# Attention with a two-matrix network: the multiplication by the softmax sums, moved from behind the visit to the middle of a slot

## The chip, the cores and the metric

The kernel runs on one core of one Trainium2 chip. The metric is device time in microseconds (us), from launch to end, of that core; lower is better. The core has five engines with instruction queues of their own: TensorE (PE; the loads of its weights are listed apart, as PEld), VectorE (DVE), ScalarE (ACT), GpSimd (POOL) and SyncE (SP), which here issues the DMAs. Each engine works through its queue in the order in which the program was written; between engines, semaphores make one wait for another.

## The reference, cut to what matters

Queries, keys and values have 8 batches, 12 heads, 448 positions and 64 numbers per head, all in float32. Queries and keys are normalised and weighted, then comes softmax attention, then a network of two matrices with `h - tanh(h)` between them:

```python
q_n, k_n = rmsnorm(q, g_q), rmsnorm(k, g_k)
scores = scale * (q_n @ k_n.T)
attn = exp(scores - max) ; attn = attn / (sum(attn) + 1e-9)
x = (attn @ v)            # as 3584 rows of 768
h = x @ w_in              # 768 x 2048
out = (h - tanh(h)) @ w_out   # 2048 x 768
```

The sum of the exponentials divides the product with the values, not the exponentials: `x` is `exp(scores) @ v`, multiplied by the sum's reciprocal.

## The kernel before, in words

The work is cut into 48 steps: step `s` is one batch `b = s // 6` and one pair of heads `hp = s % 6`. Attention of one step gives `xT`, a tile of 128 rows (64 for each of the two heads' numbers, in an order of the kernel's own) and 448 columns, the positions. Six of these tiles are a batch's input to the network.

The network of an earlier batch runs beside the attention of a later one. It is written as a generator (`mlp`), which yields after every matmul, and a function `run(ns)` takes as many of its matmuls as fill so many nanoseconds. So the order of the program is fixed when it is built: a slot of attention writes a few attention instructions, calls `run`, writes the next few, and so on. No scheduler moves anything after that.

The network multiplies with a scheme of seven products for a 2 x 2 block product (Winograd's form of Strassen's), so that its matmuls come as products of a few matmuls each, every product into one bank of PSUM. Three banks, called `mm`, serve all of them in turn. A product's bank has to be read by ScalarE or VectorE before another product may write it or add to it. In the hidden layer (`hidden`, matmuls at L841) these reads are L908 (ScalarE), L910, L912, L920, L916, L917 and L924 (VectorE), and the subtraction of the tanh, L889, on VectorE for one product in seven and on GpSimd for three. In the projection of two batches at once (`project_pair`, matmuls at L1094) they are the lines of `add`, L1101, on VectorE, and L1174, L1168 and L1108 on ScalarE; L1042 on VectorE and L1051 on GpSimd make sums of blocks of the network's activations for later products.

From step 12 on, a step is handled by `slot(s)`. It begins with a "visit": from step 13 (`FOLDED`) on, all matmuls of this step's values (L623, L635) and of the next step's scores (L569) in one go, with the exponentials (L575) on ScalarE. The visit's result lies in two banks; `divide` adds them into `xT` (ScalarE copies the first, L757; VectorE adds the second, L758) and multiplies each half of 64 rows by `rs`, the reciprocals of the sums (L762, twice). Behind the visit stand fourteen points with the network's matmuls before, between and behind them, evenly by time. At the points the slot writes what the next steps need. The first three add the exponentials of step `s + 1` (L600, L606, L613 twice, all VectorE). The fourth and fifth turn and sum them (L710, L717). The sixth scales queries and keys of step `s + 2` (L530). At the seventh stand copies on ScalarE (L725, the first half, and L501), at the eighth VectorE's transpose of the queries (L540) and the other half of L725, at the ninth the transpose of the keys (L544) and a sum (L508). The tenth has the last sums and their reciprocals (L733, L734), the twelfth and thirteenth spread and turn them into `rs` for the next slot (L741 on ScalarE, L747 on VectorE). GpSimd has the power of step `s + 2` (L523) directly behind the visit, and sums of `xT` tiles (L793, `x_sums`) in the slots of a batch's last two steps.

A slot with `hp` of 0 to 3 runs beside a hidden layer, one with 4 or 5 beside a projection; slots 28, 29, 40 and 41 are about twice as long as the others.

Of the kernel before, what the change touches and what calls it, by code (L numbers as in the profile page):

```python
# [13 lines left out]
ALU = mybir.AluOpType  # L14
# [132 lines left out]
def bounded_path(tc, ctx, q, k, v, moe_w_in, moe_w_out, out, g_col, ident, ones, half_ones, neg_half, early):  # L147
# [17 lines left out]
    nc = tc.nc  # L165
    B, H, S, D = q.shape
# [3 lines left out]
    NP = H // 2  # L170
# [328 lines left out]
    def square_blocks(s):  # L499
        sq = normed["sq", s] = late["blocks"].tile([P, 2 * S], F32, name="sum_T")  # L500
        nc.scalar.activation(  # L501
            sq, loaded["qk", s].rearrange("p i j d -> p (i j d)"), AF.Square
        )
# [31 lines left out]
    def turn_blocks(s, i):  # L535

        n = normed[s][:, i].rearrange("p j d -> p (j d)")
        if i == 0:
            qT = qkp.tile([P, S], F32, name="qT")
            nc.vector.transpose(out=qT, in_=n)  # L540
            turned[s] = qT
            return
        kT = qkp.tile([P, S], F32, name="kT")
        nc.vector.transpose(out=kT, in_=n)  # L544
        turned[s] = None, kT, turned[s]
        del normed[s]
# [5 lines left out]
    def sc_bank():  # L552
        return bank_of("sc")

    def scores(s, c, apart=False):

        rr, kT, qT = turned[s]
        n = S if c < KF else HS
        name, bufs = ("p", 2) if c < 2 else ("p_full", 1) if c < KF else ("p_last", 2)
        if c == 1:  # L560
            p = probs[s, 1] = probs[s, 0]
        else:
            p = probs[s, c] = pp.tile([P, 2, 2 if c < 2 else 1, n], F32, name=name, bufs=bufs)
        tiles = [sc_bank() for _ in range(2)]

        def score(h, i):
            at, first = (i * BL, 0) if c < KF else (i * BL % KR, i * BL // KR * n)
            r = slice(h * D, (h + 1) * D)
            nc.tensor.matmul(  # L569
                tiles[h][i * BL : (i + 1) * BL, :n], lhsT=kT[r, c * P + at : c * P + at + BL],  # L570
                rhs=qT[r, first : first + n], start=True, stop=True,
            )

        def exp(h):
            nc.scalar.activation(  # L575
                p[:, h, c if c < 2 else 0, :], tiles[h][:, :n], AF.Exp,
                scale=1.0 if rr is None else rr[:, 0, 2 * c + h : 2 * c + h + 1],
            )

        if apart:  # L580
            return [(lambda i, h=h: score(h, i), lambda h=h: exp(h)) for h in range(2)]
        for i in range(P // BL):
            for h in range(2):
                score(h, i)
        for h in range(2):
            exp(h)
# [5 lines left out]
    def add(s, now=True):  # L592

        if s <= NP + NP // 2:
            sums[s] = []
            return
        t = early["sum"]
        sums[s] = [t]
        p = full(s)
        nc.vector.tensor_tensor(out=t, in0=p[0], in1=p[1], op=ALU.add)  # L600
        if now:
            add_third(s)
# [118 lines left out]
    def gather(s, h):  # L721

        acc, part = whole[s], whole["part", s]
        for g in range(P // BL):
            nc.scalar.copy(  # L725
                out=acc[h * BL : (h + 1) * BL, g], in_=part[g * BL : (g + 1) * BL, h * NJ : (h + 1) * NJ]
            )
# [21 lines left out]
    def divide(s, av):  # L749
        b, hp = steps[s]  # L750
        rs = whole.pop(s)
        if b > PAIRED and b % 2 and hp == 1:
            x = xT[b, hp] = late["blocks"].tile([P, S], F32, name="xT_more", bufs=1)
        else:
            x = xT[b, hp] = xp.tile([P, S], F32, name="xT")
        if s >= FOLDED:
            nc.scalar.copy(out=x, in_=av[0][:, :S])  # L757
            nc.vector.tensor_tensor(out=x, in0=x, in1=av[1][:, :S], op=ALU.add)  # L758
        for m in range(2):
            rows = slice(m * D, (m + 1) * D)  # L760
            if s >= FOLDED:
                nc.vector.tensor_tensor(out=x[rows], in0=x[rows], in1=rs, op=ALU.mult)  # L762
                continue
            for n in range(2):
                nc.vector.tensor_tensor(
                    out=x[rows, n * HS : (n + 1) * HS], in0=av[n][rows, :HS], in1=rs[n * D : (n + 1) * D],
                    op=ALU.mult,
                )
        for c in range(NCH):
            del probs[s, c]  # L770
        if b < PAIRED and hp >= HC:
            c = hp - HC
            x_sums(b, (c,), range(4), nc.vector if b == 0 and c == HC - 1 else nc.gpsimd)

    def x_sums_later(s, second):
        b, hp = steps[s]
        for c in {(HC + 1, 1): (0,), (HC + 1, 2): (1,), (HC + 2, 0): (2,)}.get((hp, second), ()):
            x_sums(b, (c,), range(4), nc.gpsimd)

    def x_sums(b, chunks, which, eng):  # L780

        for c in chunks:
            x11, x12, x21, x22 = (xT[b, r][:, n : n + HS] for r in (c, c + HC) for n in (0, HS))
            for i in which:
                if i != 2 and (b, i) not in tt:
                    tt[b, i] = tp.tile([P, HC, HS], F32, name=f"tt{i}", bufs=1)
                out, a, z = (
                    lambda: (tt[b, 0][:, c], x12, x11),
                    lambda: (tt[b, 1][:, c], x22, tt[b, 0][:, c]),
                    lambda: (x12, x22, x12),  # L790
                    lambda: (tt[b, 3][:, c], x21, tt[b, 1][:, c]),
                )[i]()
                eng.tensor_tensor(out=out, in0=a, in1=z, op=ALU.subtract)  # L793


    late = {}
# [517 lines left out]
    def gap_ns(s):  # L1314

        if s < 2 * NP:
            return H_NS / 12 if s % NP < 3 else 4 * S / ENGINE_NS * CD * CF / 12
        if s < 3 * NP:
            return (H_NS + O_NS + AHEAD_NS) / (4 * NP)
        n = (s - 3 * NP) % (2 * NP)  # L1320
        return (H_NS / 16, OUTER_NS * SOON / 8, H_NS / 16, OUTER_NS * (len(OUTER) - SOON) / 8)[(n > 3) + (n > 5) + (n > 9)]

    def has(s):
        return 0 <= s < NS

    def first_slot(s):
# [31 lines left out]
        if has(s):  # L1358
            divide(s, av)
# [34 lines left out]
    def slot(s):  # L1394

        gap = gap_ns(s)
        av = av_banks
        if has(s + 1):
            scores(s + 1, KF)
        if s < FOLDED:  # L1400
            last_values(s, av)
            totals(s, sc_bank())
            divide(s, values(s, av))
            for c in range(KF):
                scores(s + 1, c)
        else:
            visit(s, av)
        if has(s + 2):
            load(s + 2, "v")
        rows, ahead, following = has(s + 2), has(s + 3), has(s + 1)  # L1410
        folded = following and s + 1 >= FOLDED
        first = s + 3 == TURNED
        scaled = rows and not first
        if scaled:
            power_blocks(s + 2)
        work = (
            (
                (following, lambda: add(s + 1, False)), (first, lambda: turn(s + 2, sc_bank(), sc_bank())),
                (ahead and not first, lambda: load_blocks(s + 3)),
            ),  # L1420
            (
                (following, lambda: add_third(s + 1)), (first, lambda: load_blocks(s + 3)),
                (True, lambda: x_sums_later(s, 0)),
            ),
            ((following, lambda: add_last(s + 1)),),
            ((folded, lambda: fold(s + 1)),),
            ((folded, lambda: fold_rest(s + 1)), (True, lambda: x_sums_later(s, 1))),
            ((scaled, lambda: scale_blocks(s + 2)),),
            ((folded, lambda: gather(s + 1, 0)), (ahead, lambda: square_blocks(s + 3))),
            ((scaled, lambda: turn_blocks(s + 2, 0)), (folded, lambda: gather(s + 1, 1))),  # L1430
            ((scaled, lambda: turn_blocks(s + 2, 1)), (ahead, lambda: norm_blocks(s + 3))),
            ((folded, lambda: spread_sums(s + 1)), (True, lambda: x_sums_later(s, 2))),
            ((scaled, lambda: weigh_keys(s + 2)), (ahead, lambda: meet_blocks(s + 3))),
            ((folded, lambda: widen_sums(s + 1)),),
            ((folded, lambda: turn_sums(s + 1)),),
            (),
        )
        for point in work:
            run(4 * gap / (len(work) + 1))
            for wanted, fn in point:  # L1440
                if wanted:
                    fn()
        run(4 * gap / (len(work) + 1))
# [358 lines left out]
```

## Time and profile before

Median of three runs: 1359.16 us (1357.87 to 1359.49). The profile is of one further execution:

| What | Value |
|---|---|
| Profiled execution, device time | 1356.19 us |
| Its span, first to last instruction | 1354.4 us |
| Granted TensorE clock over the span | 0.996 |
| TensorE, VectorE, ScalarE, GpSimd busy | 97%, 70%, 41%, 57% |
| L762, the two multiplications | 70 of them, 58.5 us |
| VectorE idle before the 35 L758 | 195 us |
| Chain that ended last | 84% TensorE, 9% VectorE, 2% DMA, 2% SyncE's queue |

In the profile's rows a line number with an engine names a group of instructions, `out<-in` are the tiles written and read, and a shape such as 64x448 is partitions by elements. Behind a bar or in square brackets stands the time in which the engine was idle before, and what ended most of that. "Waits" rows give the total in us, how many times, and the longest. Rows in order of time begin with the start and the duration in us.

### The profile page before, as it was taken

To read this page: it belongs to the slowest core of one execution; us is meant where nothing else is said; L and a number is where in the kernel's file an instruction comes from. 1 tells how busy PE (TensorE), PEld (TensorE's weight loads), DVE (VectorE), ACT (ScalarE), POOL (GpSimd) and SP (SyncE) were. 2 spreads that over 40 slices of the span, in tenths; PEclk is the share of its full clock that TensorE was granted. 3 is DMA by queue.
4 is the path that set the end of the run, shared out by engine and by line. 5 is a ranking of instruction groups with operands and counts; after the bars stand their busy time and mean duration, and the time that the engine had idled before them with its cause. 6 is when DMAs were issued, how large, how long until landed. Compare 5 with 4: busy or idle time off the path is not lost.

```text
span 1354.4 us, 29206 instructions
## 1 busy us (share of the span) xinstructions
PE 1317.9 (97%) x11336; PEld 1029.0 (76%) x11336; DVE 949.1 (70%) x1393; ACT 556.9 (41%) x1326; POOL 775.1 (57%) x591
## 2 busy tenths in 40 slices
PE   7989999999999999999999999999999999999996
PEld 3467854478998878697778787778787888699985
DVE  4999978757855768587887576768786668434453
ACT  7856654344433454445322446354512264311100
POOL 4766766347846256626698235844699253712761
PEclk9999999999999999999999999999999999999999
DMA  7879889889999667476655867476645775365544
GB/s 172 197 198 266 254 256 254 249 247 280 335 302 274 169 157 182 107 192 151 162 145 138 197 169 179 110 180 163 168 139 139 160 194 158 107 163 178 171 143 84
DMA packets 371688, 253.54 MB, mean 187 GB/s; under 512 B 282196, under 2 KB 310228, under 8 KB 371540
## 3 DMA queue, kind: packets, MB, share of 16 engines
q1 hardware_dynamic: 371536, 251.57, 68.9%
q8 instruction: 92, 1.51, 0.5%
q14 instruction: 56, 0.46, 0.1%
q10 hardware_dynamic: 4, 0.00, 0.0%
HBM read 205.23 MB, written 46.27 MB: 186 GB/s over the span
## 4 chain that ended last, share of the span: by engine, by line
PE 84%; DVE 9%; DMA 2%; SPq 2%; issue 1%; ACT 1%; POOL 1%; DVEq 0%; ACTq 0%
PE mm L841 36%; PE mm L1094 23%; PE sc L569 9%; PE sc L635 6%; PE mm L1258 5%; DVE xT L762 1%; PE sc L673 1%; PE sc L623 1%; SPq L955 1%; PE mm L673 1%; DVE rows L613 1%; DMA w_f<-w_in 1%; DVE rows L606 1%; DVE rows L600 1%; DMA w_f<-w_inner 0%
## 5 line engine op out<-in xcount | busy, mean ns | idle before, releaser
L841 PE MATMUL mm<-xT,w_f 128*128 128x224 f32 x1296 | 264.0, 353 | 0.7 <-DVE s L912 0.7
L841 PEld LDWEIGHTS mm<-xT,w_f 128*128 128x128 f32 x1296 | 244.5, 190 | 6.4 <-issue 4.8
L569 PE MATMUL sc<-qT,kT 64*32 64x448 f32 (+1 forms) x3072 | 214.2, 499 | 2.9 <-ACT p_last L575 1.7
L841 PE MATMUL mm<-tt,w_f 128*128 128x224 f32 x1044 | 213.7, 356 | 0.8 <-DMA w_f<-w_in 0.2
L841 PEld LDWEIGHTS mm<-tt,w_f 128*128 128x128 f32 x1044 | 194.9, 190 | 19.1 <-issue 15.4
L523 POOL TENSOR_TENSOR rr_mine<-rr_mine,neg_half 128x28 f32<-128x28 f32 x33 | 160.6, 4868 | 2.7
L758 DVE TENSOR_TENSOR xT<-xT,sc 128x448 f32<-128x448 f32 x32 | 19.9, 622 | 176.8 <-PE sc L569 119.3
L889 POOL TENSOR_TENSOR gT<-s,th 128x448 f32<-128x448 f32 x44 | 56.1, 1277 | 145.3 <-ACT th L888 142.0
L1094 PE MATMUL mm<-u,w_f 128*128 128x224 f32 x672 | 136.5, 354 | 1.2 <-DVE sum_all L733 0.9
L1094 PE MATMUL mm<-gT,w_f 128*128 128x224 f32 (+1 forms) x480 | 133.0, 429 | 3.1 <-DVE acc L1101 3.0
L1094 PEld LDWEIGHTS mm<-u,w_f 128*128 128x128 f32 x672 | 126.1, 190 | 8.2 <-POOL u L1051 3.9
L569 PEld LDWEIGHTS sc<-qT,kT 64*32 64x32 f32 x3072 | 71.0, 106 | 70.4 <-issue 50.5
L1094 PEld LDWEIGHTS mm<-gT,w_f 128*128 128x128 f32 x480 | 90.2, 190 | 40.7 <-issue 34.2
L635 PE MATMUL sc<-p,v_nat 64*32 64x448 f32 x1120 | 110.5, 536 | 0.0
L1094 PE MATMUL mm<-g,w_f 128*128 128x224 f32 (+1 forms) x360 | 99.5, 428 | 1.1 <-DVE acc L1101 1.1
L725 ACT COPY sum_g<-sum 32x14 f32<-32x14 f32 x280 | 56.3, 201 | 106.1 <-DVE sum L717 100.3
L889 POOL TENSOR_TENSOR g<-s,th 128x448 f32<-128x448 f32 x24 | 30.6, 1278 | 108.2 <-ACT th L888 93.3
L575 ACT ACTIVATE p<-sc 128x448 f32<-128x448 f32 x132 | 71.7, 543 | 50.3 <-PE sc L569 42.4
L1094 PEld LDWEIGHTS mm<-g,w_f 128*128 128x128 f32 x360 | 67.9, 190 | 28.2 <-issue 26.2
L1258 PE MATMUL mm<-gT,w_out 128*128 128x448 f32 x192 | 74.4, 543 | 0.0
L1051 POOL TENSOR_TENSOR u<-gT 128x448 f32<-128x448 f32 x48 | 58.8, 1247 | 11.1 <-PE mm L1094 11.1
L144 POOL TENSOR_TENSOR rr<-rr,neg_half 112x8 f32<-112x8 f32 (+1 forms) x30 | 49.4, 1675 | 26.7 <-DVE rr L143 26.2
(196 smaller groups left out, 2427.9 us busy)
## 6 DMA issues: line engine op xcount, KB each, us to landing
w_f<-w_in SPq DMA_DIRECT2D x196, 384.0 KB, 3.5
w_f<-w_inner SPq DMA_DIRECT2D x63, 512.0 KB, 3.7
w_f<-w_out SPq DMA_DIRECT2D x42, 512.0 KB, 3.9
w_raw<-in_moe_w_out_dram SPq DMA_DIRECT2D x16, 768.0 KB, 5.6
w_in<-w_out SPq DMA_DIRECT2D x21, 384.0 KB, 5.1
qk_nat<-in_q_dram SPq DMA_DIRECT2D x132, 56.0 KB, 2.8
qk_nat<-in_k_dram SPq DMA_DIRECT2D x132, 56.0 KB, 2.3
g<-w_out SPq DMA_DIRECT2D x14, 512.0 KB, 5.1
```

Of the source, the lines that this page charges most:

```text
L144: nc.gpsimd.tensor_tensor(out=r, in0=r, in1=neg_half[:rows], op=ALU.pow)
L523: nc.gpsimd.tensor_tensor(out=mine, in0=mine, in1=neg_half[:, :1].to_broadcast([P, 2 * NJ]), op=ALU.pow)
L569: nc.tensor.matmul(tiles[h][i * BL : (i + 1) * BL, :n], lhsT=kT[r, c * P + at : c * P + at + BL], rhs=qT[r, first : first + n], start=True ...
L575: nc.scalar.activation(p[:, h, c if c < 2 else 0, :], tiles[h][:, :n], AF.Exp, scale=1.0 if rr is None else rr[:, 0, 2 * c + h : 2 * c + h ...
L635: nc.tensor.matmul(av[g][i * BL : (i + 1) * BL, :S], lhsT=v_nat[keys, h, c, m * BL : (m + 1) * BL], rhs=p[keys, h], start=first, stop=True ...
L673: nc.tensor.matmul(av[n][r : r + BL, :HS], lhsT=v_nat[:, h, c, m * BL : (m + 1) * BL], rhs=p[c][:, h, n * HS : (n + 1) * HS], start=False, ...
L725: nc.scalar.copy(out=acc[h * BL : (h + 1) * BL, g], in_=part[g * BL : (g + 1) * BL, h * NJ : (h + 1) * NJ])
L841: nc.tensor.matmul(bank[:, f * HS : (f + 1) * HS], lhsT=w[:, c * width + f, :], rhs=moving[p](c), start=(first and f == 0 and c == 0), sto ...
L889: eng.tensor_tensor(out=g[:, rows, cols], in0=h, in1=th, op=ALU.subtract)
L1051: nc.gpsimd.tensor_tensor(out=u[:, half], in0=a[:, half], in1=z[:, half], op=ALU.subtract)
L1094: nc.tensor.matmul(bank[:, :n], lhsT=w(i), rhs=mv, start=(first and i == 0), stop=(i == len(moving) - 1), skip_group_check=not first,)
L1258: nc.tensor.matmul(bank[:, :S], lhsT=w_out_row(f, n // HC)[:, n % HC * P : (n % HC + 1) * P], rhs=g[:, f, :], start=(f == 0), stop=(f == C ...
```

## The change: the two multiplications are written at the seventh and eighth point

`divide` no longer multiplies, except where `hp` is 5, a batch's last step. For all others it puts two functions, one for each half of 64 rows, on a list, and a slot's seventh and eighth point each take one from it and call it. In a batch's last step both are called at once, as before. The multiplications themselves, their tiles and all other instructions stay.

```diff
         if s >= FOLDED:
             nc.scalar.copy(out=x, in_=av[0][:, :S])
             nc.vector.tensor_tensor(out=x, in0=x, in1=av[1][:, :S], op=ALU.add)
+            for m in range(2):
+                rows = x[m * D : (m + 1) * D]
+                late.setdefault("divide", []).append(
+                    lambda rows=rows: nc.vector.tensor_tensor(out=rows, in0=rows, in1=rs, op=ALU.mult)
+                )
         for m in range(2):
             rows = slice(m * D, (m + 1) * D)
             if s >= FOLDED:
-                nc.vector.tensor_tensor(out=x[rows], in0=x[rows], in1=rs, op=ALU.mult)
+                if hp == NP - 1:
+                    divide_rows()
                 continue
...
+    def divide_rows():
+        if late.get("divide"):
+            late["divide"].pop(0)()
...
-            ((folded, lambda: gather(s + 1, 0)), (ahead, lambda: square_blocks(s + 3))),
-            ((scaled, lambda: turn_blocks(s + 2, 0)), (folded, lambda: gather(s + 1, 1))),
+            (
+                (folded, lambda: gather(s + 1, 0)), (ahead, lambda: square_blocks(s + 3)),
+                (True, divide_rows),
+            ),
+            (
+                (scaled, lambda: turn_blocks(s + 2, 0)), (folded, lambda: gather(s + 1, 1)),
+                (True, divide_rows),
+            ),
```

The points' own work of VectorE is written in this order from then on: L530 at the sixth, the first multiplication at the seventh, L540 and then the second multiplication at the eighth, L544 at the ninth.

## The prediction

> **What bounds the kernel now.** I read the page first, then who waits for whom on the weight-load queue between 300 and 1200 us (the stretch that holds every slot the diff touches), then slots in order of time. "Slot 46" is step 46: batch 7, head pair 4; offsets count from the start of its L758.
>
> ```profile
> PE 1317.9 (97%) x11336; PEld 1029.0 (76%) x11336; DVE 949.1 (70%) x1393; ACT 556.9 (41%) x1326; POOL 775.1 (57%) x591
> ```
>
> TensorE sets the end. Its 97% cannot be read as "no stalls", because ends of matmuls are modelled; the weight loads, one per matmul, show them:
>
> ```profile
> PEld mm L1094 <- DVE acc L1101: 7.0, 8, 2.1
> PEld mm L841 <- DVE gT L889: 1.4, 3, 0.5
> PEld mm L841 <- DVE s L912: 1.4, 2, 0.7
> PEld mm L841 <- DVE g L889: 1.0, 2, 0.5
> PEld mm L1094 <- DVE s L1101: 0.9, 3, 0.4
> PEld mm L841 <- DVE s L917: 0.9, 5, 0.2
> ```
>
> With L920 (0.5, 1), L600 (0.4, 2) and L1042 (0.2, 1), TensorE waited for VectorE 27 times, 13.7 us. Loads of 128x224 matmuls stand 0.19 us apart anyway, so 27 x 0.19 = 5.1 of it is no loss: 8.6 remain. After nearly each, the second matmul starts 0.10 late, some 2 us in all. So late VectorE reads of product banks cost about 10.5 us of 1354.4: the most that the change can win. The worst slot, VectorE's rows and then the weight loads':
>
> ```profile
> 1160.38 0.62 DVE L758 TENSOR_TENSOR xT<-xT,sc 128x448 f32<-128x448 f32 x1 [6.99 <-PE sc L569]
> 1161.04 2.79 DVE L762 TENSOR_TENSOR xT<-xT,rs_T 64x448 f32<-64x448 f32 x2
> 1163.85 0.39 DVE L1101 TENSOR_TENSOR acc<-mm,s 128x224 f32<-128x224 f32 x1
> 1164.16 1.60 DVE L600 TENSOR_TENSOR rows<-p 128x896 f32<-128x896 f32 x1
> ...
> 1170.77 0.35 DVE L1101 TENSOR_TENSOR acc<-mm,acc 128x224 f32<-128x224 f32 x1
> ```
> ```profile
> 1164.30 1.43 PEld L1094 LDWEIGHTS mm<-gT,w_f 128*128 128x128 f32 x8 [1.05 <-DVE acc L1101]
> 1166.17 2.94 PEld L1094 LDWEIGHTS mm<-u,w_f 128*128 128x128 f32 x16 [0.45 <-issue]
> 1171.17 0.30 PEld L1094 LDWEIGHTS mm<-gT,w_f 128*128 128x128 f32 x2 [2.06 <-DVE acc L1101]
> ```
>
> VectorE has idled 7 us for the visit, then gets a burst. L1101 reads a bank filled before the visit, but stands behind the two L762; three times TensorE waits for a bank (the 0.45, called "issue", starts as the L1101 of 1165.68 ends). In a hidden-layer slot, one more read matters:
>
> ```profile
> 618.63 1.27 DVE L762 TENSOR_TENSOR xT<-xT,rs_T 64x448 f32<-64x448 f32 x2
> 633.45 0.61 DVE L917 TENSOR_TENSOR s<-mm,s 128x448 f32<-128x448 f32 x1
> ```
> ```profile
> 626.80 0.30 PEld L841 LDWEIGHTS mm<-xT,w_f 128*128 128x128 f32 x2 [0.74 <-DVE s L912]
> 629.47 2.19 PEld L841 LDWEIGHTS mm<-tt,w_f 128*128 128x128 f32 x12 [0.48 <-DVE g L889]
> 634.11 0.68 PEld L841 LDWEIGHTS mm<-tt,w_f 128*128 128x128 f32 x4 [0.18 <-DVE s L917]
> ```
>
> Here VectorE never idles from L758 to L917, and TensorE goes on as L917 ends.
>
> **What the Trainium skill says.** "SBUF — State Buffer", Who interferes with whom: a VectorE instruction with two SBUF inputs contends with a GpSimd one that reads SBUF, one with a single SBUF input does not. The trace agrees: L762 takes 0.62 alone and 1.3 to 1.6 beside GpSimd's L1051 or L1005, L600 1.09 or 1.60; L910, one input in PSUM, stays 0.62 beside L1051. The long power of L523 does not slow them: slot 34's L600 took 1.08 under it. "PSUM — Partial Sum Buffer", Engine vs sequencer instructions: VectorE's queue is strictly in order; the burst above shows it. "Perfetto Trace Analysis", Identifying the Most-Contended Engine: matmul busy share is no measure of headroom; the stalls under 97% agree.
>
> **The change, part by part.** Nothing is removed or added: 70 L762 before and after. Six slots of the 35 are a batch's last and keep theirs; 29 x 2 = 58 move behind L530 and behind L540 (in long projection slots among the L1042). The other four engines' order does not change; no DMA moves. Two GpSimd sums (L793) gain a wait on VectorE.
>
> At the old place everything up to L530 moves up by the pair's time, 1.3 us where GpSimd is quiet, up to 3.1 where it is not. At the new place the backlog is what it was, as long as VectorE has not idled meanwhile. So a stall before the new place goes for good only if no read behind it binds, or if the pair has become cheaper there. Stalls with their restarts, taken from gaps between matmul starts over 0.19:
>
> Slot 46, 0.97 + 0.37 + 1.97 = 3.3. The first L1101 ends at 1.05 instead of 3.86, L600 takes its 1.6, the second ends at 2.9, L606 and L613 stay slow beside GpSimd, the third ends at 7.9 instead of 10.74. The product that started at 10.80 starts at 8.0, after GpSimd's last u (6.37 before) has held one by 0.4. No later read is short. Gain 2.8.
>
> Slots 22 and 34, 0.91 and 0.85: the first L1101 ends at 1.05, not 3.2; the third near 6.2, not 8.2; VectorE idles 1.2 before L747 there. Gain 1.76.
>
> Slots 28 and 40, 1.34 and 0.67. The L1101 behind three L1042 (offsets 23.4 and 23.8) comes behind an L762 too: 0.65 to 1.45 later. Its bank is needed 1.5 and 0.75 after its old end, and TensorE now comes 1.3 and 0.7 earlier. I take 1.1 and 0.2: 1.3.
>
> Slots 20, 32 and 44, 0.4 before L889 and 0.1 before L917, each. Their pairs took 2.9 beside L1051; at offsets 9 to 12 GpSimd is idle (3 to 13.7), so they take 1.24, 1.7 less, while L600 and L606 now meet L1051 and grow by 0.65. L917 comes 1.0 earlier, TensorE 0.5. Gain 1.45.
>
> Slots 26 and 38, 1.06 and 0.98: their pairs were cheap already (1.27), so L917 ends where it did and takes all of it back. Gain 0. The other 19 moved slots have no stall that an L762 makes; slot 18's L917 ends 1.2 before it is needed, slot 33's 0.6.
>
> Sum 2.8 + 1.76 + 1.3 + 1.45 = 7.3. For the reads behind point eight that come later than the hand count sees I take off 0.8 (bounds: 0, and all but slot 46's, 4.5). **Gain 6.5 us.** The profiled execution (span 1354.4, 1356.19 with what lies around) becomes 1349.7; the median shown, 3.0 above it, 1359.16 - 6.5 = 1352.7. Behind slot 46 TensorE runs 147 us of matmuls almost without a gap, so a gain there reaches the end.
>
> What the moved pair holds up: behind it stand L540, L544 and L508 (used a slot later), L920 to L924 (product banks, counted above), L733, L734 and L747 (the next sums; needed only after the next visit). ScalarE's copies for the sums wait for L717, which comes earlier. L793's second group stands at point ten: in slot 46 GpSimd reaches it at 14.78, the pair is done near 13; cost 0, and if it waited GpSimd's next u would be late by the wait, at most about 1 us.
>
> **Rivals.** *All stalls go*: TensorE wins the whole of the slots counted, 3.3 + 1.76 + 2.01 + 1.5 + 2.04 = 10.6: 1348.6. For it: the reads behind point eight often have 0.6 to 1.2 of slack. Against it: slots 26 and 38 have none. *The stalls move*: L917 and the L1101 behind L1042 take back everything except part of slot 46: gain 0 to 2.7, about 1357.7. For it: five L917 waits stand in the list already. Against: GpSimd is idle where the pair goes in slots 20, 32 and 44. *Slower*: the pair, now between L530 and L544, runs contended or meets a VectorE that idled earlier, and L917 comes late in hidden slots. The seven with no slack (20, 26, 27, 32, 38, 39, 44) lose 1.7 each and ten like slot 18 or 33 lose 0.5 to 1.1: 12 + 8 = 20, less 6 won in the projections: up to 14, as a middle value 3.5: 1362.7. It decides once the pair costs over 1.2 more in its new place. Against: in slots 26 and 32 GpSimd is idle there, from 6 or 3 to 14. *It doesn't do what it says* is excluded: the instruction order shows the move.
>
> **How the numbers follow.** Forecast (gain over 2.7, up to 9.5): 0.59, its own range 1350 to 1356. All stalls go: 0.11. They move: 0.14. Slower: 0.16. A change under 0.2%, 2.7 us, cannot be told from none. Faster 0.59 + 0.11 = 0.70, same 0.14, slower 0.16. The range leaves out a tenth at each side: it takes in nearly all of the first rival and the milder part of the slower one, 1348.3 to 1360.
>
> **What would show it.** Waits of loads for L1101 fall from 7.0 to about 2; slot 46's product of 1171.17 starts 8.0 behind its L758; L762 falls from 856 ns mean to 700 to 750, L600 rises above 1202; L889 and L912 vanish from the list and L917 stays in slots 26 and 38. It is wrong if L917, or L1101 behind L1042, grows by as much as the others fall, if L762 stays above 850, or if GpSimd waits for L762.

## The result and the profile after

The changed kernel takes 1355.24 us (median of 22 runs) against 1357.59 of the kernel before (22 runs beside it): 0.9983 of the time, 95% interval 0.9976 to 0.999. That is 2.35 us less, where the prediction had 6.5. Its profiled span is 1352.9 us, 1.5 less. (One of the 22 runs of the kernel before took 1692.89; without it the median is 1357.38.) From here on a line number of the changed kernel is 10 higher than the same statement's in the kernel before, from L793 on: L917 is L927, L889 is L899, L912 is L922, L1042 is L1052, L1051 is L1061, L1101 is L1111; L762, L600, L606 and L613 keep theirs.

The page's first part, as after:

```profile
PE 1315.2 (97%) x11336; PEld 1030.8 (76%) x11336; DVE 958.5 (71%) x1393; ACT 559.0 (41%) x1326; POOL 792.8 (59%) x591
```

No instruction was added, yet VectorE is busy 9.4 us longer (949.1 before) and GpSimd 17.7 (775.1 before). So some work takes longer: the first sign that the move changed what runs beside what. The waits on the weight-load queue between 300 and 1200 us, of the changed kernel:

```profile
PEld mm L1104 <- POOL u L1061: 7.4, 9, 1.2
...
PEld mm L851 <- DVE s L927: 2.9, 2, 1.5
PEld mm L1104 <- DVE acc L1111: 1.9, 3, 1.5
PEld mm L1104 <- DVE s L1111: 1.3, 3, 0.6
PEld mm L851 <- DVE xT L762: 0.9, 1, 0.9
...
PEld mm L851 <- DVE g L899: 0.5, 2, 0.3
```

The same view of the kernel before has, beside the lines that the prediction showed, these of GpSimd:

```profile
PEld mm L1094 <- POOL u L1051: 3.7, 5, 0.7
PEld mm L1094 <- POOL g L889: 1.6, 2, 0.8
PEld mm L1094 <- POOL rr_mine L520: 1.5, 2, 0.7
```

The large wait, 7.0 for the `acc` of L1101, is down to 1.9, and L912 is gone. Two others took part of it. The wait for L917's statement grew from 0.9 to 2.9, all of it now in two places, slots 26 and 38. The wait for GpSimd's `u` grew from 3.7 to 7.4. Of that, 1.5 is a change of name: in slots 22 and 34 the wait of 0.73, as the network's loads resume behind the visit, stood under L520 before. The other 2.3 are new, in slots 28 and 40. The 1.6 under GpSimd's L889, in slots 27 and 39, is L917's too: in slot 27 of the kernel before L917 ends at 655.46 and the load starts at 655.57, while L889 had ended at 654.90.

Waits alone do not give the loss, so I use one ledger for every kernel here: the gaps between the starts of successive network matmuls beyond their usual spacing (0.19 us for 128x224, 0.38 for 128x448), summed by slot. The 0.10 us by which the second matmul behind every visit starts late, before and after, is left out. A slot's length is the distance from its L758 to the next. Before, the stalls of slots 13 to 47 sum to about 13.5 us, after to 2.8 less. (The span has only 1.5 of these 2.8: the profiled execution after is 0.8 later at slot 13 already, ahead of everything that was moved, and 0.5 longer behind slot 47.) By slot, lengths in us:

| Slots | Before | After | Gain | Predicted gain |
|---|---|---|---|---|
| 46 | 23.56 | 21.67 | 1.9 | 2.8 |
| 22, 34 | 23.09, 23.00 | 22.18, 22.15 | 1.76 | 1.76 |
| 20, 32, 44 | 22.05, 21.97, 21.97 | 21.52, 21.50, 21.50 | 1.47 | 1.45 |
| 28, 40 | 48.41, 47.82 | 48.15, 48.21 | -0.13 | 1.3 |
| 26, 38 | 22.65, 22.64 | 23.07, 23.14 | -0.92 | 0 |
| 23, 35 (keep their pair) and 27, 39 | 22.48, 22.54; 22.30, 22.18 | 22.68, 22.71; 22.37, 22.24 | -0.5 | -0.8, as the allowance |

These sum to 3.6. Another 0.8 is lost in three slots: slot 14 loses 0.39 and slot 42 0.81, while slot 30 gains 0.40. In slot 30 of the kernel before, and in slot 42 of the changed one, a matmul starts 0.135 us behind the landing of a transfer of weights. The wait above for L762 is this place in slot 42. Such late weights stand now in one slot and now in another.

Slot 14 looks like another in the first profile of the changed kernel, where one matmul starts 0.135 behind a landing. But a second profile of that kernel loses the same 0.39 there, without that late matmul. VectorE's pair before, then VectorE, GpSimd and the load of the second profile:

```profile
334.21 1.27 DVE L762 TENSOR_TENSOR xT<-xT,rs_T 64x448 f32<-64x448 f32 x2
```
```profile
346.42 1.69 DVE L762 TENSOR_TENSOR xT<-xT,rs_T 64x448 f32<-64x448 f32 x1
...
349.21 1.74 DVE L762 TENSOR_TENSOR xT<-xT,rs_T 64x448 f32<-64x448 f32 x1
350.97 0.63 DVE L899 TENSOR_TENSOR gT<-mm,th 128x448 f32<-128x448 f32 x1
```
```profile
345.51 6.57 POOL L1015 TENSOR_TENSOR g<-g 128x512 f32<-128x512 f32 x4
```
```profile
351.65 0.86 PEld L851 LDWEIGHTS mm<-tt,w_f 128*128 128x128 f32 x5 [0.34 <-DVE gT L899]
```

The pair took 0.62 for each half behind the visit. At its new place it meets GpSimd's L1015 and takes 3.4 us. L899, the read behind it, ends late, and the load waits for it. So this loss is the move's own. It is the one slot where TensorE waits because the moved pair has itself become dearer.

Slot 46 of the changed kernel in order of time, VectorE and then the weight loads:

```profile
1160.30 0.62 DVE L758 TENSOR_TENSOR xT<-xT,sc 128x448 f32<-128x448 f32 x1 [6.88 <-PE sc L569]
1160.84 0.38 DVE L1111 TENSOR_TENSOR acc<-mm,s 128x224 f32<-128x224 f32 x1
1161.14 1.70 DVE L600 TENSOR_TENSOR rows<-p 128x896 f32<-128x896 f32 x1
...
1163.06 1.72 DVE L606 TENSOR_TENSOR rows<-rows,p_full 128x896 f32<-128x896 f32 x1
1164.82 2.91 DVE L613 TENSOR_TENSOR rows<-rows,p_last 64x448 f32<-64x448 f32 x2
...
1168.80 0.35 DVE L1111 TENSOR_TENSOR acc<-mm,acc 128x224 f32<-128x224 f32 x1
```
```profile
1164.68 3.03 PEld L1104 LDWEIGHTS mm<-u,w_f 128*128 128x128 f32 x16
1169.21 0.30 PEld L1104 LDWEIGHTS mm<-gT,w_f 128*128 128x128 f32 x2 [1.49 <-DVE acc L1111]
```

The burst behind the visit has lost its L762, and the first L1111 follows L758 at once. But the three sums of exponentials now take 6.3 us for 5.3 before: they moved beside GpSimd's `u`. The third L1111 ends 8.85 behind L758 (10.74 before), and the product waits 1.49 instead of 2.06.

Slot 26 shows the opposite sign. Before, its L606 and L613:

```profile
621.47 1.50 DVE L606 TENSOR_TENSOR rows<-rows,p_full 128x896 f32<-128x896 f32 x1
623.00 2.09 DVE L613 TENSOR_TENSOR rows<-rows,p_last 64x448 f32<-64x448 f32 x2
```

After, with GpSimd and the weight load that waits:

```profile
620.14 1.08 DVE L606 TENSOR_TENSOR rows<-rows,p_full 128x896 f32<-128x896 f32 x1
621.26 2.92 DVE L613 TENSOR_TENSOR rows<-rows,p_last 64x448 f32<-64x448 f32 x2
...
629.42 0.61 DVE L762 TENSOR_TENSOR xT<-xT,rs_T 64x448 f32<-64x448 f32 x1
...
631.13 0.62 DVE L762 TENSOR_TENSOR xT<-xT,rs_T 64x448 f32<-64x448 f32 x1
...
633.83 0.62 DVE L927 TENSOR_TENSOR s<-mm,s 128x448 f32<-128x448 f32 x1
```
```profile
620.37 3.33 POOL L1061 TENSOR_TENSOR u<-g 128x448 f32<-128x448 f32 x2
```
```profile
634.50 0.68 PEld L851 LDWEIGHTS mm<-tt,w_f 128*128 128x128 f32 x4 [1.47 <-DVE s L927]
```

The pair is cheap where it went, 0.61 and 0.62. Ahead of it, both halves of L613 now lie beside GpSimd's two L1061 (620.37 to 623.70), where before L606 and one half did. L927 therefore ends 16.5 behind L758 instead of 16.1, and every stall that vanished earlier in the slot comes back there, with more.

In slot 28 the wait changes its engine. GpSimd and the load, of the changed kernel:

```profile
683.20 4.46 POOL L1061 TENSOR_TENSOR u<-g,u 128x448 f32<-128x448 f32 x2
```
```profile
687.71 0.68 PEld L1104 LDWEIGHTS mm<-u,w_f 128*128 128x128 f32 x4 [1.15 <-POOL u L1061]
```

Before, that pair of `u` ran earlier and was shorter, and the same product's load followed without a wait:

```profile
681.39 4.01 POOL L1051 TENSOR_TENSOR u<-g,u 128x448 f32<-128x448 f32 x2
```

In the changed kernel VectorE's L762, between two L1052, stands beside it:

```profile
684.11 1.55 DVE L762 TENSOR_TENSOR xT<-xT,rs_T 64x448 f32<-64x448 f32 x1
```

GpSimd came late to the pair as well: its power, L523, begins 5.2 behind L758 for 4.2 before. VectorE's rows now come earlier and meet GpSimd's work at the slot's start: the `u` there took 3.11 for 2.63, the sum L520 1.09 for 0.62.

### The profile page after: what moved, and what is told of

Read it like the earlier page. It is cut to its first block, busy times and chain, and to the rows that moved or that the text cites. A ratio compares the mean times of both kernels' runs of the same rounds, so it can differ in the third digit from the quotient of the medians.

```text
span 1352.9 us, 29209 instructions
## 1 busy us (share of the span) xinstructions
PE 1315.2 (97%) x11336; PEld 1030.8 (76%) x11336; DVE 958.5 (71%) x1393; ACT 559.0 (41%) x1326; POOL 792.8 (59%) x591
## 4 chain that ended last, share of the span: by engine, by line
PE 80%; DVE 6%; POOL 4%; DMA 3%; SPq 3%; issue 2%; ACT 1%; ACTq 0%; DVEq 0%; POOLq 0%
PE mm L851 37%; PE mm L1104 20%; PE sc L569 8%; PE sc L635 5%; PE mm L1268 5%; POOL u L1061 2%; PE sc L623 1%; PE sc L673 1%; SPq L127 1%; DMA w_raw<-in_moe_w_in_dram 1%; DVE rows L613 1%; POOL rr_mine L523 1%; DMA gT<-in_moe_w_in_dram 1%; SPq L289 1%; DMA qk_nat<-in_k_dram 1%
## 5 line engine op out<-in xcount | busy, mean ns | idle before, releaser
L523 POOL TENSOR_TENSOR rr_mine<-rr_mine,neg_half 128x28 f32<-128x28 f32 x33 | 162.7, 4931 | 2.8
L899 POOL TENSOR_TENSOR gT<-s,th 128x448 f32<-128x448 f32 x44 | 56.5, 1286 | 140.4 <-ACT th L898 140.4
L758 DVE TENSOR_TENSOR xT<-xT,sc 128x448 f32<-128x448 f32 x32 | 19.9, 621 | 167.7 <-PE sc L569 112.2
L899 POOL TENSOR_TENSOR g<-s,th 128x448 f32<-128x448 f32 x24 | 31.4, 1312 | 109.1 <-ACT th L898 109.1
L1061 POOL TENSOR_TENSOR u<-gT 128x448 f32<-128x448 f32 x48 | 65.8, 1392 | 11.1 <-PE mm L1104 11.1
```

What stands on the lines that cost most here:

```text
L523: nc.gpsimd.tensor_tensor(out=mine, in0=mine, in1=neg_half[:, :1].to_broadcast([P, 2 * NJ]), op=ALU.pow)
L899: eng.tensor_tensor(out=g[:, rows, cols], in0=h, in1=th, op=ALU.subtract)
L1061: nc.gpsimd.tensor_tensor(out=u[:, half], in0=a[:, half], in1=z[:, half], op=ALU.subtract)
```

## The experiments

My theory after this: behind the visit the move is worth what was predicted, but in hidden slots with no slack (26, 27, 38, 39) the pair at points seven and eight stands ahead of L927 and takes all back; and `u`, which contends with VectorE, makes the size of everything else. The rivals: the losses are late transfers or chance between executions; or the burst's order alone counts, not GpSimd.

The kernel before ran again beside these runs: its median is 1356.99 us beside the first four and 1357.23 beside the last three. The ratios below compare with those runs, and differ from the quotients of the medians by up to 0.0005. Each edit is a cut from the diff against the changed kernel, where nothing else is said.

**Later in hidden slots.** In steps beside a hidden layer the pair goes behind L927, to the eleventh and twelfth point. `steps[s][1]` is `hp` and `HC` is 3, so projection slots keep the seventh and eighth; the first edit stands at both.

```diff
-                (True, divide_rows),
+                (steps[s][1] > HC, divide_rows),
...
-            ((scaled, lambda: weigh_keys(s + 2)), (ahead, lambda: meet_blocks(s + 3))),
-            ((folded, lambda: widen_sums(s + 1)),),
+            ((scaled, lambda: weigh_keys(s + 2)), (ahead, lambda: meet_blocks(s + 3)), (True, divide_rows)),
+            ((folded, lambda: widen_sums(s + 1)), (True, divide_rows)),
```

> The pair of L762 of slots with head pair 0 to 3 is written at the eleventh and twelfth point, behind the reads L926 and L927 and the sums L733 and L734; slots with head pair 4 keep it at the seventh and eighth. Theory (the reads that stand behind the new place in the same queue take the gain back): without the pair in front of it, L927 ends 1.2 us earlier, so slots 26 and 38 fall from 23.07 and 23.14 us to about 21.6, 27 and 39 from 22.3 to about 21.6, and 20, 32 and 44 stay at 21.5. That is 4.4 us less than in the changed kernel: about 1351, 0.995 of the time before. Rival (the loss in 26 and 38 is made at the slot's start, where L606 and L613 now meet GpSimd's sums, wherever the pair goes): they fall by less than 0.4 us each and the time stays near 1355, 0.998.

Measured: 1349.14 us, 0.9947 of the kernel before (0.9933 to 0.996). Slots 26 and 38 have no stall left (21.49 and 21.57), nor have 27 and 39 (21.59 and 21.46). VectorE in slot 26:

```profile
630.48 0.61 DVE L927 TENSOR_TENSOR s<-mm,s 128x448 f32<-128x448 f32 x1
...
631.43 0.55 DVE L762 TENSOR_TENSOR xT<-xT,rs_T 64x448 f32<-64x448 f32 x1
...
632.54 0.92 DVE L762 TENSOR_TENSOR xT<-xT,rs_T 64x448 f32<-64x448 f32 x1
```
```profile
631.18 0.76 PEld L851 LDWEIGHTS mm<-tt,w_f 128*128 128x128 f32 x4
```

With L758 at 616.28, L927 ends 14.8 behind it, not 16.5, and the load of `tt` waits for nothing. Of these 1.7 us about 1.2 are the two L762 that no longer stand ahead. Most of the rest is that L606 and L613 take 3.60 together instead of 4.00: GpSimd's `u` starts 1.6 behind L758 there, not 2.4, and meets L606 and one half of L613 as it did before. Slots 28 and 40 are as in the changed kernel (48.14, 48.22), as they should be. Slot 14, whose pair is late too, is back at 27.11, its length before. This takes away the rival of chance: a place in the program made the loss. (Slot 42 loses 1.1 to late weights in this profile.)

**The move in six slots only**, those where the ledger says it gains.

```diff
-                if hp == NP - 1:
+                if s not in (20, 22, 32, 34, 44, 46):
                     divide_rows()
```

> The pair moves to the seventh and eighth point in slots 20, 22, 32, 34, 44 and 46 alone; all others keep it behind the visit. Theory (slots add up, and what each won in the trace it wins alone): 0.5 + 0.9 + 0.5 + 0.85 + 0.5 + 1.9 = 5.1 us less than before, about 1352.5, 0.996. Rival (what a slot wins is lost again later, because TensorE only meets the next late transfer or read sooner): no better than the full change, 0.998.

Measured: 1352.52 us, 0.9966 (0.9956 to 0.9977), 4.5 us less than before; those six slots are 4.9 us shorter. Slots 26, 28, 38 and 40 have their lengths of before. The profiled execution, 1354.04, shows how large chance is: slots 14 and 17 lose 0.64 and 1.16 to late weights in it, ahead of slot 20, the first whose order differs from the kernel before.

**The move in the other six only**: the condition is `s not in (26, 27, 28, 38, 39, 40)`.

> The pair moves in slots 26, 27, 28, 38, 39 and 40 alone. Theory (these are the slots in which the move loses): 26 and 38 grow by 0.4 to 0.5, 27 and 39 by 0.06, 28 falls by 0.3 and 40 grows by 0.4: 1.2 us more than before, 1.0009, with the loads' waits for L927 above 2.5 us in all. Rival (the losses of the changed kernel's profile are chance of one execution): the six slots as before within 0.2 us in all, 1.0000.

Measured: 1359.92 us, 1.0027 (1.0016 to 1.0037). The six slots lose 1.2 together, as expected, and the waits of the load queue have it:

```profile
PEld mm L1104 <- POOL u L1061: 5.9, 7, 1.1
...
PEld mm L851 <- DVE s L927: 3.5, 5, 1.5
```

The median is 1.7 beyond the expectation. In its profile, an execution of 1358.55, late weights in slot 42 cost 0.55, and the stretch behind the last L758 is 0.8 longer than in the profile of the kernel before. (That one has the shortest such stretch: the other profiles here have 0.3 to 1.2 more.) The profiled execution is 1.4 below the median; that remainder I could not place.

**The changed kernel once more**, unaltered.

> The changed kernel once more, with a second profile. Theory: 0.998 again, and slots 26, 38 and 46 within 0.1 us of 23.07, 23.14 and 21.67. The stalls of slots 14 (0.39) and 42 (0.81), which stand in no row of VectorE's that the move made later, are gone or elsewhere if they belong to that one execution; they come again if the move made them.

Measured: 1353.73 us, 0.9978 (0.997 to 0.9986). Slots 26, 38 and 46 are 23.06, 23.14 and 21.70: what I explain repeats within 0.03. Slot 42, where a transfer was late, has 0.13 instead of 0.81. Slot 14 has its 0.39 again. By the expectation's own test the move made that one, and the rows of L762, L1015 and L899 above show how.

**Without the computation of `u`**, on the kernel before and on the changed one. GpSimd writes a constant into the tile instead of the difference of two tiles; the subtraction is left out, so only times count. This takes away both the contention and most of the time that GpSimd spends.

```diff
-            nc.gpsimd.tensor_tensor(out=u[:, half], in0=a[:, half], in1=z[:, half], op=ALU.subtract)
+            nc.gpsimd.memset(u[:, half], 0.0)
```

> The kernel before, but GpSimd sets the block sums u to zero instead of subtracting (L1051 becomes a memset): it leaves out their computation, and reads no SBUF there. Theory (the stalls behind the visit come from VectorE's two-input rows being slowed by those reads, with the pair in front): the pair takes 1.24 us, L606 1.08 and L613 0.62 each, the third L1101 of slot 46 ends at 7.4 instead of 10.74, and slots 20, 22, 26, 32, 34, 38 and 46 have almost no stall left: 26 and 38 near 21.6 us, 46 near 20.2 (before 22.65, 22.64, 23.56). Slots 27 and 39, whose rows were never slowed, keep their 0.7. Rival (the order of the queue alone makes the stalls): at least half of each remains, slot 46 above 21.8.

> The changed kernel with the same edit: u set to zero, its computation left out. Theory: slots 26, 38 and 46 near 21.6 and 20.2 us here too, so that the move is worth less than 0.5 us over slots 20 to 46; L613 takes 0.62 (1.43 and 1.46 in slot 26 of the changed kernel). Rival (the loss in 26 and 38 is the move's own, from the second multiplication between L540 and L544 and not from slowed rows): they stay 0.4 above the kernel before with the same edit.

Measured, one run each: 1350.83 us with the old order, 1349.43 with the new (spans 1349.0 and 1347.6). The stalls of slots 20, 26, 28, 32, 38, 40 and 44 are gone in the old order already: they were GpSimd's. Slots 22 and 34 keep 0.78 and 0.71 in the old order and have none in the new: those two are the order's alone, which my expectation denied. Slot 14 is 27.11 in the old order and 27.52 in the new, so that loss does not need `u` either. In slot 46 the old order leaves this (VectorE, then the loads):

```profile
1156.98 1.27 DVE L762 TENSOR_TENSOR xT<-xT,rs_T 64x448 f32<-64x448 f32 x2
...
1159.89 1.25 DVE L606 TENSOR_TENSOR rows<-rows,p_full 128x896 f32<-128x896 f32 x1
1161.17 1.96 DVE L613 TENSOR_TENSOR rows<-rows,p_last 64x448 f32<-64x448 f32 x2
...
1164.21 0.35 DVE L1101 TENSOR_TENSOR acc<-mm,acc 128x224 f32<-128x224 f32 x1
```
```profile
1164.61 0.30 PEld L1094 LDWEIGHTS mm<-gT,w_f 128*128 128x128 f32 x2 [0.87 <-DVE acc L1101]
```

and the new one none:

```profile
1163.69 0.38 PEld L1104 LDWEIGHTS mm<-gT,w_f 128*128 128x128 f32 x2
```

Slot 46 is 21.05 in the old order and 20.25 in the new. Its third read ends 8.2 behind L758 in the old order, where 7.4 was expected. So of its 3.4 us of stalls before, about 2.5 needed `u` beside VectorE. The new order also loses nothing in 26 and 38 here (21.49, 21.57): with quiet sums L927 is early enough even with the pair ahead of it. What the order is worth without `u` is 0.78 + 0.71 + 0.80 = 2.3 us in these three slots, where I had expected under 0.5. (Slots 23 and 35 are longer without `u` than with it, 22.96 and 23.0, in both orders; why was not followed.) In slot 46 L613 stays slow without `u` as well, 0.96 and 0.97, beside GpSimd's L793.

**Later in slots 28 and 40 too**, pair at the eleventh and twelfth point, and the second group of L803 behind it, at the thirteenth; as a diff to the first experiment.

```diff
-                (steps[s][1] > HC, divide_rows),
+                (s in (16, 22, 34, 46), divide_rows),
...
-            ((folded, lambda: spread_sums(s + 1)), (True, lambda: x_sums_later(s, 2))),
+            ((folded, lambda: spread_sums(s + 1)), (s not in (28, 40), lambda: x_sums_later(s, 2))),
...
-            ((folded, lambda: turn_sums(s + 1)),),
+            ((folded, lambda: turn_sums(s + 1)), (s in (28, 40), lambda: x_sums_later(s, 2))),
```

> The run with the late pair, with slots 28 and 40 late too: there the pair is written at the eleventh and twelfth point and the second group of L803, which reads its result, at the thirteenth. Theory (in these two slots the pair among the L1052 slows GpSimd's L1061, and TensorE waits 1.0 us for its u at offset 24): that wait goes, 28 and 40 fall from 48.14 and 48.22 us to about 47.2, and the time to about 1347, 0.993. Rival (GpSimd is late there because of the power L523, which now begins 0.9 us later, whatever the pair does): the wait stays at 0.7 or more and the slots change by less than 0.4.

Measured: 1348.67 us, 0.9937 (0.9923 to 0.995), not to be told from 0.9947. Both slots fell by 0.52 (to 47.62 and 47.69), not to 47.2, and the load's wait for `u` from about 1.06 to 0.54. The pair of `u`:

```profile
680.20 3.92 POOL L1061 TENSOR_TENSOR u<-g,u 128x448 f32<-128x448 f32 x2
```

So L762 beside it made half of that wait (4.46 against 3.92). The other half remains, and with it GpSimd's lateness at the slot's start: L523 begins 5.1 behind L758 here too. That this lateness is the whole of the other half is argued, not tried. Slots 29 and 41 each give 0.35 back, and slot 30 loses 1.0 to late weights in this profile. This kernel and that of the first experiment, 0.5 to 0.6% faster than the kernel before, are the best found.

## Why the prediction came out as it did

**The bound and the size of the prize** held. All stalls, GpSimd's among them, were about 13.5 by the ledger, and the best kernels recover about 8 of them; the prediction's ceiling was 10.5. Its list of 27 waits left out slots 27 and 39, 0.7 each, which stood under GpSimd's L889. It counted both among the slots without a stall that an L762 makes. With the pair behind L917's statement both stalls are gone (21.59 and 21.46), so an L762 made them.

**Slots 22 and 34** (1.76) and **20, 32 and 44** (1.45) came out at 1.76 and 1.47. The reasons hold as well: with `u` gone the first two keep their stall in the old order, the other three lose it.

**Slot 46** (2.8): the mechanism was right, the term for the sums too small. The step said that L606 and L613 stay as slow as before and that L600 takes its 1.6. L600 and L606 did (1.70 and 1.72). L613, moved forward into `u`, took 2.91 for the two, not 1.97. That 0.94 is nearly all of the miss: the third read ends at 8.85, not 7.9, the product starts at 8.9, not 8.0.

**Slots 26 and 38** (0) failed at the sentence that their pairs were cheap already, so that L917 "ends where it did". The pair is as cheap, but the step looked at the pair only. In front of it L613 moved into GpSimd's 3.3 us of `u`, and L917's statement ends 0.42 later. The same contention had been counted for L600 and L606 in 20, 32 and 44, and not here. Putting the pair behind this read wins 3.2 us in the two slots, as the first experiment shows.

**Slots 28 and 40** (1.3) failed at the limit chosen: I searched the next late read on VectorE, the L1101 behind three L1042. It was GpSimd's L1051, 24.3 behind L758, whose pair is slowed by the L762 and L1042 beside it and starts later as well. The prediction priced what GpSimd does to VectorE, and not what VectorE does to GpSimd. With `u` left out the wait goes, with L762 elsewhere half of it: so the engine is shown, and L762's share.

**The allowance of 0.8** was near: slots 23, 27, 35 and 39 lost 0.5, and slot 14 lost 0.39. That the sum fits is luck in part: the allowance was for reads behind point eight that come later, and slot 14 failed at the price of the pair, 3.4 us for 1.24, which the prediction did not look up there.

So 7.3 - 0.8 = 6.5 became 3.6 by slots: 0.9 went in slot 46, 1.4 in 28 and 40, 0.9 in 26 and 38, and 0.3 came back from the allowance. Slot 14 took 0.39 of the rest in the profiled execution, and late weights, which no step had, 0.4 (0.81 lost in slot 42, 0.40 gained in slot 30).

The time, 1355.24, does lie between 1350 and 1356, but that is luck. The range was counted from 1359.16, and the kernel before took 1357.59 beside the changed one; with the gain at little over a third of 6.5, it is this lower start that puts the time into the range.

**The rivals.** The gain of 2.35 us lies just under the forecast's own limit of 2.7 and inside the band of "the stalls move". That rival had one of its two mechanisms right: L917 in 26 and 38 grew; the L1101 behind L1042 did not. "All stalls go" fell with 26 and 38. "Slower" asked for a pair that costs over 1.2 more at its new place: it costs 0.61 and 0.62 in slot 26, and what was added there stands ahead of it. In slot 14 alone that price was passed, by 2.2, and TensorE lost 0.39. So this rival was right in one slot out of 29.

**The signs named in advance.** The wait for the `acc` of L1101 fell to 1.9 (about 2 expected). L912 vanished, L889 all but 0.5. L917 stayed in 26 and 38, and grew to 2.9. GpSimd's only wait for L762 became shorter, 5.5 for 7.6. Means of two groups, between 300 and 1200 us of the changed kernel, were off:

```profile
L613 DVE TENSOR_TENSOR rows<-rows,p_last 64x448 f32<-64x448 f32 x68 | 52.1, 766 | 1.8
L762 DVE TENSOR_TENSOR xT<-xT,rs_T 64x448 f32<-64x448 f32 x64 | 51.7, 808 | 1.1
L600 DVE TENSOR_TENSOR rows<-p 128x896 f32<-128x896 f32 x34 | 42.8, 1258 | 0.1
```

L762 fell from 856 to 808 only (700 to 750 expected), since it still runs beside GpSimd's work in slots 22, 28, 34, 40 and 46, and newly in 14 and 15. L600 rose from 1202, as said. L613, which was on no list, rose from 709 to 766: 57 ns more for each of 68, 3.9 us in all. This mean was the sign to have watched.

## What to carry to other kernels

When instructions are moved out of a burst, all that stood behind them moves forward: price each of these against what the other engine runs at its new time, not the moved pair alone, and in both directions. Then find, for each kind of slot, the last read that has no slack, and put the moved work behind it: here that turned 0.2% into 0.5 to 0.6%. A wait list should be read for all engines, since a wait removed on one can return on another under another name.

## What was not expected of the hardware

The Trainium skill, "SBUF — State Buffer", Who interferes with whom, says that a VectorE instruction with two SBUF inputs contends with a GpSimd instruction that reads SBUF, and not with one that only writes it. (What it says of a single SBUF input, taken up in the prediction, it says only outside VectorE's 2-port performance modes.) The runs without `u` agree: in slot 26 of the new order L606 took 1.08 with both of the constant's writes beside it, and in slot 46 too it took 1.08 (1.72 beside the subtraction).

The price of overlap, which decided this case, had to be read from rows. Half an L613 went from 0.62 to about 1.44, L606 from 1.08 to as much as 1.72; on the other side GpSimd's two halves of `u`, 2.26 in a quiet place of the changed kernel, took 3.33 beside L606 and L613 in slot 26. Behind these prices is a pattern. Slot 46 of the changed kernel, GpSimd and VectorE by single instructions:

```profile
1163.79 1.98 POOL L1061 TENSOR_TENSOR u<-gT,u 128x448 f32<-128x448 f32 x1
1164.82 1.44 DVE L613 TENSOR_TENSOR rows<-rows,p_last 64x448 f32<-64x448 f32 x1
1165.74 1.51 POOL L1061 TENSOR_TENSOR u<-gT,u 128x448 f32<-128x448 f32 x1
1166.29 1.45 DVE L613 TENSOR_TENSOR rows<-rows,p_last 64x448 f32<-64x448 f32 x1
1167.21 1.05 POOL L803 TENSOR_TENSOR tt<-xT 128x224 f32<-128x224 f32 x1
```

The two engines take turns. Each L613 ends 0.48 behind the end of GpSimd's half, and the half between them ends 1.00 behind an L613. Alone they take 0.62 and 1.13, so an instruction that waits for its turn ends some 0.13 to 0.14 less than its own time behind the other's end. This is so in every such row of the changed kernel from 300 us on: of those that took over 0.06 more than alone, all 14 L613 end 0.48 and all 16 L600 and L606 end 0.95 behind the end of a GpSimd instruction. With this the loss could have been priced from ends alone: in slot 46 before, an L613 met GpSimd's L793, of half the columns, and after it met halves of `u`.

GpSimd's power L523, on 28 columns, did not slow VectorE: L600 and L606 in slot 28 of the kernel before took 1.08 each, wholly inside its 5.60. That the power itself takes 4.80 us ahead of slot 26 of the changed kernel and 5.58 in slot 28 is seen in the trace; why was not tried.
